# The last 128 output columns of a Mish layer: one cast and one store, or two of each by halves of the partitions

## The chip, the cores and the metric

The kernel runs on one core of a Trainium2 chip. The metric is the device time of one execution in microseconds (us). Each kernel is run several times, and the median is compared; beside these runs one execution is recorded by the hardware profiler.

## The reference

The layer takes `x` (2048 tokens by 512), `w1` (512 by 1792), `b1` (1792) and `w2` (1792 by 512), all in bf16:

```
h   = x @ w1 + b1
act = h * tanh(softplus(h))      # Mish
out = act @ w2                   # 2048 x 512, bf16
```

## The kernel before

The tokens are worked in four blocks of 512 (`BLOCKS`). For each block there are two stages on TensorE:

- First product (`mm1_step`, line 164). For each of 14 groups of 128 hidden features, four matrix products of 512 columns accumulate in one bank of PSUM, the accumulator memory of eight banks. ScalarE reads the bank, applies Mish with the bias and writes `a_sb` in bf16 (`mish`, line 170).
- Second product (`mm2`, line 197). For each of the four groups of 128 tokens in the block (index `i`, 0 to 15 over the whole kernel), 14 matrix products over the hidden features accumulate up to 512 output columns in one bank.

What follows a second product is `put`. One engine waits for the last of the 14 products, reads the bank and writes the result in bf16 to `o_sb`: VectorE at line 185, or, if the queue given is ScalarE's, ScalarE at line 182. Then a DMA is issued at line 189, from SP for VectorE's casts and from ScalarE for its own. SP and ScalarE have a DMA ring each (q1 and q10 in the profile). Every store adds 16 to the one semaphore `s_out`.

The order is written out by hand; there is no planner. All engines run their own instruction lists and wait on counting semaphores; `Stream.wait` leaves out a wait that is already known to be met. SP first issues all the loads (line 85) and then only the stores. ScalarE issues two loads at the start, then works 56 times Mish, then the last cast.

The last group of tokens, `i = 15`, is split: 512 - `LAST` = 416 columns go through VectorE and SP's ring, and the last `LAST` = 96 columns, with 14 products of their own in another bank, go through ScalarE and its ring. At the very end SP waits for all 17 stores (line 234).

Of the kernel before, what the change touches and what calls it, by code (L numbers as in the profile page):

```python
# [5 lines left out]
P = 128  # L6
WARM = (512,) * 5 + (128,) * 5
BLOCKS = (512, 512, 512, 512)
LAST = 96


class Stream:
# [20 lines left out]
def bass_standalone__dense_activation_mish__prompt_kernel(  # L33
# [8 lines left out]
    ACT = mybir.ActivationFunctionType  # L42
# [3 lines left out]
    _, S, D = x.shape  # L46
# [3 lines left out]
    x2, out2 = x[0], out[0]  # L50
# [5 lines left out]
    with ExitStack() as es:  # L56
        def sb(name, shape, t):
            return es.enter_context(nc.sbuf_tensor(name, shape, t))
# [12 lines left out]
        o_sb = sb("o_sb", [P, S // P, D], BF)  # L71
        ps = es.enter_context(nc.psum_tensor("ps", [P, 8, 512], F32))

        def sem(name):
            return es.enter_context(nc.semaphore(name))

        sp = Stream(nc.sync, None)
        pe = Stream(nc.tensor, sem("c_pe"))
        dve = Stream(nc.vector, sem("c_dve"))
        act = Stream(nc.scalar, sem("c_act"))  # L80
# [29 lines left out]
        out01 = out2[0:2 * P, :].rearrange("(p j) d -> p j d", j=2)  # L110
# [24 lines left out]
        free = [[] for _ in range(8)]  # L135
# [19 lines left out]
        def mm1_step(s, f, k, bank, j0=0, j1=None):  # L155
            j1 = BLOCKS[s] // P if j1 is None else j1
            lo, hi = j0 * P, j1 * P
            first = k == 0 and j0 == 0
            if first:
                pe.wait(*free[bank])  # L160
            pe.wait(t_w1[k, f])
            for j in range(starts[s] // P + j0, starts[s] // P + j1):
                pe.wait(t_cp[k] if j < 2 else t_xT[j])
            return nc.tensor.matmul(ps[:, bank, lo:hi], w1_sb[:, k, f * P:(f + 1) * P],  # L164
                                    xT[:, k, starts[s] + lo:starts[s] + hi], start=first,
                                    stop=(k == KT - 1 and hi == BLOCKS[s]))

        def mish(s, f, bank, t_mm):
            act.wait(t_b1c, t_mm)
            t = act.mark(act.eng.activation(a_sb[:, f, starts[s]:starts[s + 1]], ps[:, bank, 0:BLOCKS[s]], ACT.Mish,  # L170
                                            bias=b1_sb[:, f:f + 1]))
            t_mish[s, f] = t
            free[bank] = [t]

        s_out = sem("s_out")
        n_out = 0

        def put(i, lo, hi, bank, t_mm, q):
            nonlocal n_out
            if q is act:  # L180
                act.wait(t_mm)
                t = act.mark(act.eng.activation(o_sb[:, i, lo:hi], ps[:, bank, 0:hi - lo], ACT.Copy))  # L182
            else:
                dve.wait(t_mm)
                t = dve.mark(nc.vector.tensor_copy(o_sb[:, i, lo:hi], ps[:, bank, 0:hi - lo]))  # L185
            free[bank] = [t]
            q.wait(t)
            dst = out01[:, i, lo:hi] if i < 2 else out2[i * P:(i + 1) * P, lo:hi]
            q.eng.dma_start(dst, o_sb[:, i, lo:hi]).then_inc(s_out, 16)
            n_out += 1  # L190

        def mm2(i, lo, hi, bank, q=sp):
            s = max(b for b in range(len(BLOCKS)) if starts[b] <= i * P)
            pe.wait(*free[bank])
            for f in range(FT):
                pe.wait(t_w2[f], t_mish[s, f])
                mm = nc.tensor.matmul(ps[:, bank, 0:hi - lo], a_sb[:, f, i * P:(i + 1) * P], w2_sb[:, f, lo:hi],  # L197
                                      start=(f == 0), stop=(f == FT - 1))
            put(i, lo, hi, bank, pe.mark(mm), q)


        for n in WARM:
# [14 lines left out]
        for f in range(F0):  # L217
            for k in range(KT):
                mm = mm1_step(0, f, k, f, 2, 4)
            mish(0, f, f, pe.mark(mm))  # L220

        for s in range(len(BLOCKS)):
            for f in range(F0 if s == 0 else 0, FT):
                bank = f % 8 if s == 0 else 4 + f % 4
                for k in range(KT):
                    mm = mm1_step(s, f, k, bank)
                mish(s, f, bank, pe.mark(mm))
            for i in range(starts[s] // P, starts[s + 1] // P):
                if i < S // P - 1:
                    mm2(i, 0, D, i % 4)  # L230
                else:
                    mm2(i, 0, D - LAST, i % 4)
                    mm2(i, D - LAST, D, (i + 1) % 4, act)
        sp.eng.wait_ge(s_out, 16 * n_out)


# [26 lines left out]
```

## Time and profile before

| what | us |
|---|---|
| median of three runs | 105.71 |
| the three runs | 105.72, 105.71, 105.05 |
| the profiled execution, whole time | 104.98 |
| its span, first to last instruction | 103.7 |
| TensorE busy in the span | 100.9 (97%) |
| VectorE busy | 13.2 (13%) |
| ScalarE busy | 38.9 (38%) |
| TensorE's granted clock, mean | 1.000 |

The span is shorter than the whole time by what lies before the first and behind the last instruction that the profile shows. Rows of the profile name an engine by PE (TensorE), PEld (its weight loads), DVE (VectorE), ACT (ScalarE), POOL (GpSimd) and SP (SyncE); "SPq" and "ACTq" are DMA issues by the queues of SP and ScalarE. "L185" is line 185 of the kernel. "128x416 bf16<-128x416 f32" means 128 partitions by 416 elements, read as f32 and written as bf16. The time of a DMA issue is that of the issuing instruction; its "landing" is when its semaphore has been raised in full.

### The profile page before, as it was taken

The numbers are of one execution on the slowest core, as the hardware profiler recorded it, in microseconds if no ns is written. First come the engines' busy times: TensorE is split into PE (matmuls) and PEld (weight loads), VectorE is DVE, ScalarE is ACT, GpSimd is POOL, SyncE is SP. The second block draws the span as 40 slices with busy tenths as digits, with TensorE's granted clock in tenths as the row PEclk, the third lists the DMA queues.
The fourth block names the chain that finished last, engine by engine and source line by source line (L and its number), as shares of the span: only waits on it lengthen the run. The fifth ranks groups of instructions, "written<-read, shape, count | busy, mean of one in ns | idle before, by whom it ended". The sixth has DMA issues, their size and how long they took to land.

```text
span 103.7 us, 1167 instructions
## 1 busy us (share of the span) xinstructions
PE 100.9 (97%) x512; PEld 49.8 (48%) x512; DVE 13.2 (13%) x26; ACT 38.9 (38%) x58; POOL 0.7 (1%) x6
## 2 busy tenths in 40 slices
PE   6999999999999999999999999999999999999992
PEld 2788744444444444444444444444444444444451
DVE  0430000212220000022220000022211000021122
ACT  1305997000037777100007777400006777700000
POOL 2000000000000000000000000000000000000000
PEclk9999999999999999999999999999999999999999
DMA  1999995992110000011011000001111000001111
GB/s 54 355 303 354 350 254 123 231 241 69 51 45 6 0 6 0 0 51 47 4 51 51 0 0 0 9 0 51 51 51 51 0 0 0 0 6 51 51 51 51
DMA packets 12865, 7.94 MB, mean 77 GB/s; under 512 B 7868, under 2 KB 12220, under 8 KB 12860
## 3 DMA queue, kind: packets, MB, share of 16 engines
q1 hardware_dynamic: 12544, 7.58, 27.6%
q10 hardware_dynamic: 316, 0.29, 0.9%
q8 instruction: 4, 0.07, 0.3%
q14 instruction: 1, 0.01, 0.0%
HBM read 3.94 MB, written 2.10 MB: 58 GB/s over the span
## 4 chain that ended last, share of the span: by engine, by line
PE 97%; ACT 0%; issue 0%
PE ps L164 47%; PE ps L197 47%; PE ps L133 3%; PE ps L145 1%; ACT o_sb L182 0%
## 5 line engine op out<-in xcount | busy, mean ns | idle before, releaser
L170 ACT ACTIVATE a_sb<-ps,b_sb 128x512 bf16<-128x512 f32 x56 | 37.4, 692 | 49.6 <-PE ps L164 49.6
L164 PE MATMUL ps<-xT,w_sb 128*128 128x512 bf16 (+1 forms) x256 | 49.5, 355 | 0.0
L197 PE MATMUL ps<-w_sb,a_sb 128*128 128x512 bf16 (+2 forms) x238 | 49.0, 366 | 0.0
L164 PEld LDWEIGHTS ps<-xT,w_sb 128*128 128x128 bf16 x256 | 25.2, 99 | 23.5
L197 PEld LDWEIGHTS ps<-w_sb,a_sb 128*128 128x128 bf16 x238 | 22.7, 98 | 26.1
L185 DVE CAST o_sb<-ps 128x512 bf16<-128x512 f32 (+1 forms) x16 | 11.0, 685 | 84.5 <-PE ps L197 84.5
L182 ACT ACTIVATE o_sb<-ps 128x96 bf16<-128x96 f32 x1 | 0.2, 250 | 11.4 <-PE ps L197 11.4
L133 PE MATMUL ps<-const-bfloat16-1.0 128*128 128x512 bf16 (+1 forms) x10 | 2.8, 466 | 0.8 <-PEq L248 0.8
L133 PEld LDWEIGHTS ps<-const-bfloat16-1.0 128*128 128x128 bf16 x10 | 1.2, 139 | 2.2 <-issue 2.2
L127 ACT ACT_TABLE_LOAD x1 | 1.3, 1283 | 2.1 <-issue 2.1
L149 DVE COPY xT<-ps 128x256 bf16<-128x256 bf16 (+1 forms) x3 | 0.9, 336 | 3.1 <-PE ps L145 2.9
L145 PE MATMUL ps<-ident,x_nat 128*128 128x128 bf16 x8 | 1.0, 309 | 0.0
L211 DVE STREAM_TRANSPOSE b_t<-b_pad 32x32 bf16<-32x32 bf16 x4 | 0.8, 202 | 0.1
L145 PEld LDWEIGHTS ps<-ident,x_nat 128*128 128x128 bf16 x8 | 0.8, 139 | 0.1
L125 POOL TENSOR_SCALAR_AFFINE_SELECT ident<-ones 128x128 bf16<-128x128 bf16 x1 | 0.3, 292 | 0.1
L106 DVE MEMSET b_pad<- 32x64 uint32 x1 | 0.1, 112 | 0.9 <-PEq L248 0.9
L123 POOL MEMSET ones<- 128x128 bf16 x1 | 0.2, 204 | 0.3 <-POOLq L248 0.3
L208 DVE COPY b_pad<-b_nat 14x128 bf16<-14x128 bf16 x1 | 0.2, 182 | 0.0
L213 DVE CAST b_sb<-b_t 128x14 f32<-128x14 bf16 x1 | 0.2, 175 | 0.0
L248 POOL MEMSET const-bfloat16-1.0<- 128x1 bf16 x1 | 0.1, 101 | 0.0
L248 POOL MEMSET const-uint8-127<- 128x1 uint8 x1 | 0.1, 101 | 0.0
L248 POOL MEMSET const-float32-0.0<- 128x1 f32 x1 | 0.1, 98 | 0.3 <-issue 0.3
(1 smaller groups left out, 0.1 us busy)
## 6 DMA issues: line engine op xcount, KB each, us to landing
out_dram<-o_sb SPq DMA_DIRECT2D x15, 128.0 KB, 1.7
w_sb<-in_w_dram SPq DMA_DIRECT2D x1, 1152.0 KB, 11.7
w_sb<-in_w_dram SPq DMA_DIRECT2D x3, 256.0 KB, 4.3
w_sb<-in_w_dram SPq DMA_DIRECT2D x2, 384.0 KB, 5.3
w_sb<-in_w_dram SPq DMA_DIRECT2D x1, 640.0 KB, 7.2
x_nat<-in_x_dram SPq DMA_DIRECT2D x1, 256.0 KB, 2.6
w_sb<-in_w_dram ACTq DMA_DIRECT2D x1, 256.0 KB, 3.1
out_dram<-o_sb SPq DMA_DIRECT2D x1, 104.0 KB, 1.7
```

The costliest lines, as they stand in the source:

```text
L123: t_ones = pool.mark(pool.eng.memset(ones[:, :], 1.0))
L125: t_id = pool.mark(pool.eng.affine_select(ident[:, :], ones[:, :], pattern=[[1, P]], compare_op=ALU.is_equal, fill=0.0, base=0, channel_mu ...
L127: act.eng.preload_act_table(ACT.Mish)
L133: nc.tensor.matmul(ps[:, 7, 0:n], c_w, c_m[:, 0:n], start=True, stop=True)
L145: mm = nc.tensor.transpose(psb[:, (2 * i + j) * P:(2 * i + j + 1) * P], x_nat[:, j, k * P:(k + 1) * P], ident[:, :])
L149: t = dve.mark(nc.vector.tensor_copy(xT[:, ks[0]:ks[0] + n, 0:2 * P], psb[:, 0:2 * n * P].rearrange("p (k t) -> p k t", k=n)))
L164: return nc.tensor.matmul(ps[:, bank, lo:hi], w1_sb[:, k, f * P:(f + 1) * P], xT[:, k, starts[s] + lo:starts[s] + hi], start=first, stop=( ...
L170: t = act.mark(act.eng.activation(a_sb[:, f, starts[s]:starts[s + 1]], ps[:, bank, 0:BLOCKS[s]], ACT.Mish, bias=b1_sb[:, f:f + 1]))
L185: t = dve.mark(nc.vector.tensor_copy(o_sb[:, i, lo:hi], ps[:, bank, 0:hi - lo]))
L197: mm = nc.tensor.matmul(ps[:, bank, 0:hi - lo], a_sb[:, f, i * P:(i + 1) * P], w2_sb[:, f, lo:hi], start=(f == 0), stop=(f == FT - 1))
L211: t_b1t = dve.mark(nc.vector.transpose(b1_t[c * 32:(c + 1) * 32, :], b1_pad[:, c * 32:(c + 1) * 32]))
L248: nc = _bacc.Bacc("TRN2", target_bir_lowering=False, num_devices=1)
```

## The change

`LAST` becomes 128, so the last group of tokens is split into 384 and 128 columns. `put` now takes the casting engine, the issuing queue and a range of partitions. For the last 128 columns (`mm2_halves`) VectorE casts partitions 0 to 63 and SP stores them; ScalarE casts partitions 64 to 127 and stores them from its own ring. All other parts (`mm2_whole`) go through VectorE and SP as before. Each ring has a semaphore of its own, and at the end SP waits for its 17 stores and ScalarE for its one.

```
-LAST = 96
+LAST = 128
...
-        s_out = sem("s_out")
-        n_out = 0
-
-        def put(i, lo, hi, bank, t_mm, q):
-            nonlocal n_out
-            if q is act:
-                act.wait(t_mm)
-                t = act.mark(act.eng.activation(o_sb[:, i, lo:hi], ps[:, bank, 0:hi - lo], ACT.Copy))
-            else:
-                dve.wait(t_mm)
-                t = dve.mark(nc.vector.tensor_copy(o_sb[:, i, lo:hi], ps[:, bank, 0:hi - lo]))
-            free[bank] = [t]
-            q.wait(t)
-            dst = out01[:, i, lo:hi] if i < 2 else out2[i * P:(i + 1) * P, lo:hi]
-            q.eng.dma_start(dst, o_sb[:, i, lo:hi]).then_inc(s_out, 16)
-            n_out += 1
+        s_out = {sp: sem("s_out_sp"), act: sem("s_out_act")}
+        n_out = {sp: 0, act: 0}
...
-            put(i, lo, hi, bank, pe.mark(mm), q)
+            return pe.mark(mm)
+
+
+        def put(eng, q, i, a, b, lo, hi, bank, t_mm):
+            eng.wait(t_mm)
+            to, src = o_sb[a:b, i, lo:hi], ps[a:b, bank, 0:hi - lo]
+            t = eng.mark(eng.eng.activation(to, src, ACT.Copy) if eng is act else eng.eng.tensor_copy(to, src))
+            q.wait(t)
+            dst = out01[:, i, lo:hi] if i < 2 else out2[i * P:(i + 1) * P, lo:hi]
+            q.eng.dma_start(dst[a:b, :], to).then_inc(s_out[q], 16)
+            n_out[q] += 1
+            return t
+
+        def mm2_whole(i, lo, hi, bank):
+            free[bank] = [put(dve, sp, i, 0, P, lo, hi, bank, mm2(i, lo, hi, bank))]
+
+
+        def mm2_halves(i, lo, hi, bank):
+            t_mm = mm2(i, lo, hi, bank)
+            put(dve, sp, i, 0, P // 2, lo, hi, bank, t_mm)
+            put(act, act, i, P // 2, P, lo, hi, bank, t_mm)
...
-                    mm2(i, 0, D, i % 4)
+                    mm2_whole(i, 0, D, i % 4)
                 else:
-                    mm2(i, 0, D - LAST, i % 4)
-                    mm2(i, D - LAST, D, (i + 1) % 4, act)
-        sp.eng.wait_ge(s_out, 16 * n_out)
+                    mm2_whole(i, 0, D - LAST, i % 4)
+                    mm2_halves(i, D - LAST, D, (i + 1) % 4)
+        for q in (sp, act):
+            q.eng.wait_ge(s_out[q], 16 * n_out[q])
```

More of the change, by code (lines that the diff above doesn't have):

```diff
@@ L173, in mish, with mm2 @@
             free[bank] = [t]
-        s_out = sem("s_out")
-        n_out = 0
-        def put(i, lo, hi, bank, t_mm, q):
-            nonlocal n_out
-            if q is act:
-                act.wait(t_mm)
-                t = act.mark(act.eng.activation(o_sb[:, i, lo:hi], ps[:, bank, 0:hi - lo], ACT.Copy))
-            else:
-                dve.wait(t_mm)
-                t = dve.mark(nc.vector.tensor_copy(o_sb[:, i, lo:hi], ps[:, bank, 0:hi - lo]))
-            free[bank] = [t]
-            q.wait(t)
-            dst = out01[:, i, lo:hi] if i < 2 else out2[i * P:(i + 1) * P, lo:hi]
-            q.eng.dma_start(dst, o_sb[:, i, lo:hi]).then_inc(s_out, 16)
-            n_out += 1
-        def mm2(i, lo, hi, bank, q=sp):
+        s_out = {sp: sem("s_out_sp"), act: sem("s_out_act")}
+        n_out = {sp: 0, act: 0}
+        def mm2(i, lo, hi, bank):
             s = max(b for b in range(len(BLOCKS)) if starts[b] <= i * P)
```

## The prediction

> **What bounds the kernel now.** I read the summary page first: its table of engines, then the chain that ended last.
>
> ```profile
> span 103.7 us, 1167 instructions
> ...
> PE 100.9 (97%) x512; PEld 49.8 (48%) x512; DVE 13.2 (13%) x26; ACT 38.9 (38%) x58; POOL 0.7 (1%) x6
> ...
> PE 97%; ACT 0%; issue 0%
> ```
>
> TensorE is busy from the first microsecond to the last two, and 97% of the chain is TensorE. The change adds no matrix product and takes none away, so only the tail behind the last product can move. The chain in order of time names where the tail begins, and the timeline of the last microseconds shows it piece by piece (columns: start, length, then engine, line, operation):
>
> ```profile
> 89.62 12.14 PE ps L197 x70
> 101.75 0.02 issue
> 101.78 0.25 ACT o_sb L182
> ```
>
> ```profile
> 95.70 0.69 DVE L185 CAST o_sb<-ps 128x512 bf16<-128x512 f32 x1 [2.33 <-PE ps L197]
> 98.72 0.69 DVE L185 CAST o_sb<-ps 128x512 bf16<-128x512 f32 x1 [2.33 <-PE ps L197]
> 101.18 0.59 DVE L185 CAST o_sb<-ps 128x416 bf16<-128x416 f32 x1 [1.77 <-PE ps L197]
> 101.78 0.25 ACT L182 ACTIVATE o_sb<-ps 128x96 bf16<-128x96 f32 x1 [11.43 <-PE ps L197]
> 101.80 0.33 SPq L189 DMA_DIRECT2D out_dram<-o_sb  x1
> 102.06 0.37 ACTq L189 DMA_DIRECT2D out_dram<-o_sb  x1
> ```
>
> The reader should see two short chains. The 416 columns are cast by VectorE from 101.18 and stored from SP at 101.80; the last 96 are cast by ScalarE from 101.78 and stored from ScalarE's own ring at 102.06. Which one ends the kernel is in the list of DMA issues (last column: us from issue to landing), and SP's own wait list shows that it stands at the final wait:
>
> ```profile
> out_dram<-o_sb SPq DMA_DIRECT2D x15, 128.0 KB, 1.7
> out_dram<-o_sb SPq DMA_DIRECT2D x1, 104.0 KB, 1.7
> out_dram<-o_sb ACTq DMA_DIRECT2D x1, 24.0 KB, 1.6
> ```
>
> ```profile
> SPq L234 <- DMA out_dram<-o_sb: 1.5, 1, 1.5
> ```
>
> SP's store lands at 101.80 + 1.7 = 103.50, ScalarE's at 102.06 + 1.6 = 103.66; the span ends at 103.7. So the 96-column chain sets the end, by some 0.16 us, and the tail is 103.7 - 101.78 = 1.92 us, of which 1.6 is a store of only 24 KB. That is the whole stage that the change can touch: 1.8% of the time.
>
> **Part 1, the split 384 + 128 instead of 416 + 96.** Does TensorE finish at another time? The 14 products of 416 columns run from the release of the cast at 98.72 to that of the cast at 101.18: 2.46 us, 0.176 each. The 14 of 96 run from there to 101.78: 0.60, 0.043 each. That is (0.176 - 0.043)/320 = 0.416 ns a column, so 14 x 384 cost 14 x 0.162 = 2.27 and 14 x 128 cost 14 x 0.056 = 0.79, together 3.06: what 2.46 + 0.60 gave. The last product still releases its readers at 101.78. Term: 0.00. The cast of the wide part now begins 0.18 us sooner, at 101.00.
>
> For its length the groups kept apart by shape serve (busy, mean ns):
>
> ```profile
> L185 DVE CAST o_sb<-ps 128x512 bf16<-128x512 f32 x15 | 10.4, 691 | 82.7 <-PE ps L197 82.7
> L185 DVE CAST o_sb<-ps 128x416 bf16<-128x416 f32 x1 | 0.6, 592 | 1.8 <-PE ps L197 1.8
> L170 ACT ACTIVATE a_sb<-ps,b_sb 128x512 bf16<-128x512 f32 x56 | 37.4, 692 | 49.6 <-PE ps L164 49.6
> L182 ACT ACTIVATE o_sb<-ps 128x96 bf16<-128x96 f32 x1 | 0.2, 250 | 11.4 <-PE ps L197 11.4
> L208 DVE COPY b_pad<-b_nat 14x128 bf16<-14x128 bf16 x1 | 0.2, 182 | 0.0
> ```
>
> VectorE: (691 - 592)/96 = 1.03 ns a column, hence 559 ns for 384: done at 101.56, 0.22 us ahead of the last product. This cover matters, since VectorE now has a second cast to do at 101.78. SP issues the wide store at 101.59 (0.03 behind its cast, as 101.80 stands behind 101.77) and is free at 101.92, ahead of its second store. Even if the wide part were back at 416 columns, VectorE would be free at 101.77, just in time. Landing at 101.59 + 1.7 = 103.29, it is off the path.
>
> **Part 2, the last 128 columns by halves.** Removed: one ScalarE cast of 128 x 96 and its store of 24 KB. Added: a VectorE cast and a ScalarE cast of 64 partitions x 128 columns, and a store of 16 KB on each ring. No row shows a cast of half the partitions. VectorE by columns: 592 - 288 x 1.03 = 295 ns. Bounds: 182 (the smallest copy of 128 columns above, 14 partitions) and 592. I take 295, because the 14-partition copy is no shorter in proportion to its partitions. ScalarE: (692 - 250)/416 = 1.06 ns a column gives 284; bounds 250 and 284 (the slope mixes two functions). So the halves are ready at 102.07 (VectorE) and 102.06 (ScalarE), and their stores issue at 102.10 and 102.09, against 102.06 before. Term: **+0.04**, by the later one. Behind the waiting casts nothing is queued on either engine but the store and the end. Half the partitions buy no shorter cast; the extra 32 columns cost that term.
>
> **Part 3, the two small stores.** DMA activity in 40 slices of 0.05 us, from 99.4 on for a lone 128 KB store (issued at 99.44), then from 101.7 on for the last two stores together:
>
> ```profile
> 99.44 0.33 SPq L189 DMA_DIRECT2D out_dram<-o_sb  x1
> ```
>
> ```profile
> GB/s 0 0 0 0 0 0 0 0 0 0 0 0 0 0 0 0 0 123 225 348 348 451 389 369 226 123 21 0 0 0 0 0 0 0 0 0 0 0 0 0
> ...
> q1 hardware_dynamic: 144, 0.13, 18.8%
> ```
>
> ```profile
> GB/s 0 0 0 0 0 0 0 0 0 0 0 0 0 0 0 0 0 0 83 183 266 366 333 349 304 283 215 148 77 16 0 0 0 0 0 0 0 0 0 0
> ...
> q1 hardware_dynamic: 144, 0.11, 16.2%
> q10 hardware_dynamic: 144, 0.02, 6.3%
> ```
>
> The lone store moves bytes from 100.25 to 100.75, 0.81 behind its issue; its packets fill 18.8% of 2.0 us, 0.38, so 0.12 of the 0.50 is the engines' uneven start. It lands 0.4 behind the last byte. The small ScalarE store, issued at 102.06, starts at about 102.87 by the same 0.81 and the last byte goes at 103.20: 0.33, of which its own packets fill 6.3% of 2.0, 0.13, and the uneven start 0.12. Some 0.08 is left for sharing the engines with the 104 KB. In the changed kernel the wide store begins 0.21 sooner, moves bytes from 102.40 to about 102.87, and is nearly gone when the halves begin at 102.90. Each half has 64 rows of 256 B instead of 128 of 192. Passing one behind the other they fill at least the 0.13 and at most a third more, 0.17 (same row count, longer rows); side by side, half of that. I take them one behind the other, the dearer case, at its middle 0.15. With the start's 0.12 that is 0.27 instead of 0.33: **-0.06**. Bounds: -0.14 (side by side) and 0.00 (no sharing relieved).
>
> By the Trainium skill, "DMA: Bandwidth & Descriptors", section "Rules for kernel authors", two transfers to disjoint partition halves serialize, as both spread over the same 16 engines, and one full transfer is advised. By that rule the term stays at -0.06; were the halves independent it would be -0.14. No row of this run has two equal halves in flight.
>
> **Part 4, a semaphore per ring.** SP waits for 17 stores, ScalarE for one. This adds a wait at the end of ScalarE's queue with nothing behind it but the program's end. Term 0.00 while ScalarE's end is covered by SP's; without that cover see the third rival.
>
> **Sum:** 0.00 + 0.04 - 0.06 + 0.00 = -0.02 us. The profiled execution took 104.98 (span 103.7 and 1.28 around it), so 104.96 for it. That execution is 0.73 under the median of the runs, 105.71, whose spread is 105.05 to 105.72. The step of -0.02 is put on the median: **105.7**.
>
> **Rivals.** (1) *The two issues exclude each other.* The stores issue 0.01 apart, on SP and on ScalarE. If the second waits until the first is done, it is late by 0.33 (SP's issue in the timeline): 105.71 - 0.02 + 0.33 = 106.0. For it: ScalarE's issue took 0.37 where it overlapped SP's by 0.07. Against it, the start of the kernel:
>
> ```profile
> 0.80 0.39 SPq L85 DMA_DIRECT2D x_nat<-in_x_dram  x1
> ...
> 1.01 0.38 ACTq L85 DMA_DIRECT2D w_sb<-in_w_dram  x1
> ```
>
> There two issues overlapped by 0.18 and each lost only some 0.05. The Trainium skill, "Perfetto Trace Analysis", section "DMA Instruction — HWDGE (DVE, Sync)", has the descriptor generator shared and locked by one sequencer at a time; by a full lock this rival holds.
>
> (2) *Small stores land sooner.* If a lone small store pays only the 0.81 before its first byte and the 0.4 behind its last, with 0.06 to 0.15 of packets between, it lands in 1.27 to 1.36 instead of 1.6: 105.71 + 0.04 - 0.33 = 105.4, or 105.5. For it: 128 KB land in 1.7, so the fixed part is most. Against it: the 24 KB took 1.6, and its end came 0.46 behind the last byte, later than for the large one.
>
> (3) *ScalarE's closing work comes onto the path.* Before, ScalarE is done at 102.43, 1.27 us ahead of the span's end; with its own wait it ends with SP. Whatever it does after its last instruction, within the 1.28 outside the span, was hidden up to those 1.27. If it takes longer than SP's, the excess is added: up to 1.27, so 106.98; at half, 106.3. It decides from about 0.1 us of excess, and passes 1% from 1.06. For it: 1.28 us outside the span are unexplained. Against it: VectorE and TensorE were done two microseconds earlier too, and closing work common to all engines is already paid by the last, SP.
>
> (4) *The halves are not cast side by side.* If two engines cannot read one bank of the accumulators at once, the second half comes 0.28 later: 106.0. No row has two engines in one bank, so nothing speaks for or against but the many casts beside running products in other banks.
>
> **How the numbers follow.** Forecast 0.58, rivals 0.16, 0.14, 0.08 and 0.04. A measurement of this kernel tells about 1%, 1.06 us, from no change. Forecast and rivals 1, 2 and 4 all lie within it. Slower by over 1% is the upper part of the third: 0.04. Faster by over 1% needs rival 2 at its full 0.3 together with all three runs at the low end of the spread (-0.66): 0.02. The rest, 0.94, is the same. Range: from 104.9 (the lowest run, 105.05, less the 0.14 of part 3 at its best) to 106.1 (the highest, 105.72, and 0.33 of late issue). Left out: most of rival 3.
>
> **What would show it.** Right: VectorE casts 384 columns in 0.56 from 101.00; both 64 x 128 casts begin at 101.78, taking 0.30 and 0.28; stores issue at 102.09 and 102.10; the wide store lands near 103.3; the span stays 103.6 to 103.8 with 1.28 around it. Wrong: an issue or first byte on one ring 0.3 behind the other (rival 1); landings at 1.4 or less (2); an unchanged span with a longer time (3); casts one behind the other (4). A product row longer than 0.056 of spacing for 128 columns would break part 1.

## The result and the profile after

| | before | changed |
|---|---|---|
| median of 21 runs each, us | 105.05 (104.52 to 105.79) | 105.67 (105.25 to 106.41) |
| profiled execution, us | 104.98 | 105.53 |
| its span, us | 103.7 | 104.1 |
| time less span, over all runs, us | 1.20 to 1.32 | 1.36 to 1.47 |

The ratio is 1.0061 with a 95% interval of 1.0037 to 1.0085: the changed kernel is slower by 0.64 us, between 0.39 and 0.89. That is under 1%, yet clear of no change. The forecast was -0.02 us. Its 105.7 agrees with the measured 105.67 only by chance: it was put on a median of three runs, 105.71, which stood 0.66 above the median of the longer series. The step is what was forecast wrongly. (The time outside the span of the kernel before is taken from the 35 runs of the first series of experiments. Spans are kept to 0.1 us, so each time outside, and each tail below, is good to about 0.05.) The prediction took 1.06 us for the least that a measurement tells from no change; with 21 runs each it is about 0.25, so the miss shows. Of the experiments below, the profiled executions of kernels 1 and 5 stalled inside the span (607 and 276.5 us); of the first no row is used, of the second only rows behind its last product.

The timeline of the changed kernel's tail (start, length, engine, line, operation), and SP's last issue by itself, as the row at 101.53 merges both of SP's issues:

```profile
100.95 0.56 DVE L191 CAST o_sb<-ps 128x384 bf16<-128x384 f32 x1 [1.58 <-PE ps L183]
101.53 1.05 SPq L194 DMA_DIRECT2D out_dram<-o_sb  x2
101.73 0.27 ACT L191 ACTIVATE o_sb<-ps 64x128 bf16<-64x128 f32 x1 [11.43 <-PE ps L183]
101.73 0.28 DVE L191 CAST o_sb<-ps 64x128 bf16<-64x128 f32 x1 [0.22 <-PE ps L183]
102.03 0.56 ACTq L194 DMA_DIRECT2D out_dram<-o_sb  x1
```

```profile
102.04 0.55 SPq L194 DMA_DIRECT2D out_dram<-o_sb  x1
```

Up to the two issues everything stands where it was expected: the last product releases both casts at 101.73, they take 0.28 and 0.27, and the stores are issued at 102.04 and 102.03. Before, the one store issued at 102.06. But the issues, SP's and ScalarE's, now take 0.55 and 0.56 instead of 0.33 and 0.37. The list of DMA issues of this stretch (last column: us to landing), and the DMA activity in 40 slices of 0.05 us from 102.2 on, show what follows:

```profile
out_dram<-o_sb SPq DMA_DIRECT2D x1, 96.0 KB, 1.6
out_dram<-o_sb ACTq DMA_DIRECT2D x1, 16.0 KB, 2.0
out_dram<-o_sb SPq DMA_DIRECT2D x1, 16.0 KB, 1.8
```

```profile
GB/s 0 0 0 123 246 338 369 369 308 154 62 0 0 0 0 0 0 0 0 0 26 92 108 82 21 0 82 103 93 46 5 0 0 0 0 0 0 0 0 0
```

The slices show three separate hills. The wide store moves bytes from 102.35 to 102.75. Then nothing moves for 0.45 us. SP's half follows from 103.20, 1.16 behind its issue, and ScalarE's from 103.50, 1.47 behind. Before, the first byte came 0.81 behind. No hill touches another, so the engines that move the bytes are not what is short.

The tail, from the start of the casts that the last product releases to the end of the span, was 103.7 - 101.78 = 1.92 us and is 104.1 - 101.73 = 2.37. This measure is used for all kernels below, since the span alone also holds the start of the kernel, which varies: these casts start anywhere from 101.4 to 102.6 in the profiles of kernels 2 to 4 and 6 to 9. Outside the span the profiled executions add 105.53 - 104.1 = 1.43 after and 104.98 - 103.7 = 1.28 before, another 0.15. So 0.45 + 0.15 = 0.60 us are to be explained.

### The profile page after: what moved, and what is told of

It is laid out like the page before. It is cut to its first block, busy times and chain, and to the rows that moved or that the text cites. A ratio compares the mean times of both kernels' runs of the same rounds, so it can differ in the third digit from the quotient of the medians.

```text
span 104.1 us, 1170 instructions
## 1 busy us (share of the span) xinstructions
PE 100.9 (97%) x512; PEld 49.9 (48%) x512; DVE 13.4 (13%) x27; ACT 38.9 (37%) x58; POOL 0.7 (1%) x6
## 4 chain that ended last, share of the span: by engine, by line
PE 97%; DVE 0%; issue 0%
PE ps L164 47%; PE ps L183 46%; PE ps L133 3%; PE ps L145 1%; DVE o_sb L191 0%
## 5 line engine op out<-in xcount | busy, mean ns | idle before, releaser
L191 DVE CAST o_sb<-ps 128x512 bf16<-128x512 f32 (+2 forms) x17 | 11.2, 660 | 84.4 <-PE ps L183 84.4
```

What stands on the lines that cost most here:

```text
L191: t = eng.mark(eng.eng.activation(to, src, ACT.Copy) if eng is act else eng.eng.tensor_copy(to, src))
```

## The experiments

The medians, ratios and tails of all kernels in one table; "outside" is the time less the span, as the range over the runs. Series ran at different times, so the ratios to the kernel before, measured beside each, are what compares.

| kernel | median us | ratio to before, 95% | tail us | outside us |
|---|---|---|---|---|
| changed kernel | 105.67 | 1.0061 (1.0037 to 1.0085) | 2.37 | 1.36 to 1.47 |
| 1 only the wait per ring | 105.34 | 1.0006 (0.9981 to 1.0031) | not read | 1.35 to 1.46 |
| 2 SP waits for both | 105.66 | 1.0052 (1.0022 to 1.0082) | 2.40 | 1.20 to 1.30 |
| 3 ScalarE later | 105.59 | 1.0050 (1.0017 to 1.0083) | 2.41 | 1.36 to 1.45 |
| 4 half casts, one store from SP | 105.09 | 0.9970 (0.9941 to 0.9999) | 1.84 | 1.19 to 1.29 |
| 5 both halves from SP | 105.75 | 1.0052 (1.0016 to 1.0088) | 2.77 | 1.22 to 1.31 |
| 6 halves by columns | 105.68 | 1.0047 (1.0019 to 1.0074) | 2.66 | 1.20 to 1.47 |
| 7 96 and 32 rows | 105.39 (one run) | none | 1.99 | 1.39 |
| 8 one cast, one store from SP | 104.96 | 0.9982 (0.9952 to 1.0013) | 1.79 | 1.21 to 1.33 |
| 8 once more | 104.92 | 0.9981 (0.9947 to 1.0016) | 1.75 | 1.22 to 1.31 |
| 9 96 and 32 rows, SP waits | 105.23 | 1.0014 (0.9985 to 1.0043) | 1.95 | 1.22 to 1.34 |

Kernels 10 and 11, below, measure single stores; they have one run each, 105.24 and 105.42.

### 1 and 2: who ends last

The first theory had two parts: two issues at the same moment on two rings get in each other's way, and the closing behind the span grows when ScalarE ends last. The first two kernels test the second part alone, from both sides. Kernel 1 is the kernel before with

```
-        s_out = sem("s_out")
+        s_out = {sp: sem("s_out_sp"), act: sem("s_out_act")}
...
-        sp.eng.wait_ge(s_out, 16 * n_out)
+        for q in (sp, act):
+            q.eng.wait_ge(s_out[q], 16 * n_out[q])
```

> The kernel before with only the semaphore per ring and ScalarE's own wait at the end. Theory (ScalarE ending last lengthens the closing outside the span): span unchanged at 103.7, the time outside the span rises from 1.27 to about 1.41, so +0.14 us in the time. Rival (the closing does not care which engine ends last; the 1.41 after the change is chance): 1.27 outside, time as before.

Kernel 2 is the changed kernel with

```
-            q.eng.wait_ge(s_out[q], 16 * n_out[q])
+            sp.eng.wait_ge(s_out[q], 16 * n_out[q])
```

> The changed kernel, but SP waits for both semaphores and ScalarE for none. Theory: the two issues still collide, both at about 0.55 us, the span stays at 104.1, and the time outside it falls back from 1.41 to 1.27: about 0.14 us faster than the change, still 0.4 slower than before. Rival (closing does not depend on the engine): no difference from the change.

The time outside the span answers it without any overlap: 1.35 to 1.46 over the 12 runs of kernel 1, 1.20 to 1.30 over the 12 runs of kernel 2. Against the medians of the kernel before, 1.26, and of the changed kernel, 1.43, adding ScalarE's wait costs 0.14 (median 1.40) and taking it away gives 0.17 back (median 1.26): about 0.15. In the time itself 0.15 us is 0.14%, which the intervals cannot tell. Kernel 6, below, whose two stores land at nearly the same moment, has both values in one program: its runs fall into two groups, six from 1.20 to 1.30 and four from 1.39 to 1.47, which fits now one ring ending last and now the other; its profiled execution, in which SP's store landed last, has 1.30. The Trainium skill, "Runtime: NRT & Kernel Launch", section "The ~15µs preamble/postamble breakdown", gives 44 ns a hop for the barrier that passes from engine to engine ahead of a kernel. It gives no hop for the barrier behind the kernel; if that one's hops are as long, an estimate from the page makes 0.15 about three of them. No run here shows the hops.

### 3 and 4: is it two issues at one moment?

Kernel 3 delays ScalarE's store by one more cast into an unused tile:

```
+        spare = sb("spare", [P, LAST], BF)
...
+            act.wait(t_mm)
+            act.eng.activation(spare[P // 2:P, :], ps[P // 2:P, bank, 0:hi - lo], ACT.Copy)
             put(act, act, i, P // 2, P, lo, hi, bank, t_mm)
```

> The changed kernel with one more cast of the same half into an unused tile ahead of ScalarE's cast, so that ScalarE's store issues about 0.28 us behind SP's instead of beside it; more work on the path, and nothing else moved. Theory (two issues at the same moment get in each other's way): SP's issue back at 0.33 and its store landing in 1.6, ScalarE's issue at 0.37 to 0.40 from 102.33, landing in 1.6 to 1.7, so the span falls to about 103.95 in spite of the added cast. Rival (a store of 64 partitions is slow by itself): issues stay at 0.55, ScalarE's landing stays near 2.05, span about 104.4.

The timeline of its last microseconds for ScalarE, SP's last issue, and the landings:

```profile
101.49 0.27 ACT L207 ACTIVATE spare<-ps 64x128 bf16<-64x128 f32 x1 [11.43 <-PE ps L184]
101.67 0.26 ACT L192 ACTIVATE o_sb<-ps 64x128 bf16<-64x128 f32 x1
101.96 0.53 ACTq L195 DMA_DIRECT2D out_dram<-o_sb  x1
```

```profile
101.81 0.55 SPq L195 DMA_DIRECT2D out_dram<-o_sb  x1
```

```profile
out_dram<-o_sb SPq DMA_DIRECT2D x1, 16.0 KB, 1.8
out_dram<-o_sb ACTq DMA_DIRECT2D x1, 16.0 KB, 1.9
```

The span, 103.9, is what the theory said, and it misleads: the last product ended 0.24 sooner in this execution. The tail is 2.41, no shorter than the change's, and both issues still take 0.55 and 0.53. The two casts overlap by 0.09, so ScalarE's issue came only 0.15 behind SP's and the two were not fully apart. The test did not separate the theories as planned, but SP's issue gave no sign of relief. The later issue cost nothing: ScalarE's first byte again comes 0.29 behind SP's (0.30 in the changed kernel), so its store had been standing behind SP's anyway.

Kernel 4 keeps the split and the half casts and joins the stores; SP alone waits at the end:

```
+            for eng, a, b in ((dve, 0, P // 2), (act, P // 2, P)):
...
+                sp.wait(t)
+            sp.eng.dma_start(out2[i * P:(i + 1) * P, lo:hi], o_sb[:, i, lo:hi]).then_inc(s_out[sp], 16)
...
+        sp.eng.wait_ge(s_out[sp], 16 * n_out[sp])
```

> The changed kernel's 384 + 128 columns and its two half casts, but one store of all 128 partitions from SP that waits for both casts; ScalarE issues none and waits for none. Theory (collision of issues): SP's last issue at 102.05 takes 0.33, lands in 1.6 to 1.7, span 103.65 to 103.75, outside 1.27, time as before or up to 0.05 less. Rival (two engines reading one bank, or the split 384 + 128, is what costs): the span stays near 104.1.

Its cast, its last issue and that store's landing:

```profile
102.56 0.28 DVE L207 CAST o_sb<-ps 64x128 bf16<-64x128 f32 x1 [0.22 <-PE ps L183]
102.92 0.33 SPq L209 DMA_DIRECT2D out_dram<-o_sb  x1
```

```profile
out_dram<-o_sb SPq DMA_DIRECT2D x1, 32.0 KB, 1.5
```

Here too the span alone, 104.4, would have pleaded for the rival; the tail, 104.4 - 102.56 = 1.84, does not. With one store of 128 rows the tail is 0.53 below the change's, while the two half casts and the columns are the same. That clears the casts and the shared bank. The rule of the Trainium skill weighed in the prediction, one full transfer rather than two halves, is borne out by the result: 32 KB in one store land in 1.5, each 16 KB half in 1.8 and 2.0. Its reason, the halves sharing the engines, could at most put the second hill behind the first. It does not explain the 0.45 us ahead of the first hill, in which the engines move nothing.

### 5, 6 and 7: two rings, or 64 rows?

Kernel 5 takes the second ring away, with its wait; kernel 6 keeps both rings but gives each store all rows; kernel 7 changes the row counts.

```
-            put(act, act, i, P // 2, P, lo, hi, bank, t_mm)
+            put(act, sp, i, P // 2, P, lo, hi, bank, t_mm)
...
+        sp.eng.wait_ge(s_out[sp], 16 * n_out[sp])
```

> The changed kernel with both 64-row stores issued from SP, one behind the other; ScalarE casts its half, issues nothing and waits for none, so that no two issues are at work at once. Theory A (a store of 64 rows is slow by itself: long issue, late first byte): both issues at 0.55 us, first byte 1.2 behind the first issue, the second store issued near 102.6 and landing 1.7 to 1.8 later, span near 104.4. Theory B (two issues at one moment get in each other's way): both issues at 0.33, landings of 1.5 to 1.6, span near 104.0. Time outside the span 1.27 in both.

```
...
+                sp.wait(t)
+                act.wait(t)
+            mid = (lo + hi) // 2
+            for q, c, d in ((sp, lo, mid), (act, mid, hi)):
+                q.eng.dma_start(out2[i * P:(i + 1) * P, c:d], o_sb[:, i, c:d]).then_inc(s_out[q], 16)
...
```

> Casts by halves as in the changed kernel, but the two stores take all 128 rows of 64 columns each, issued at the same moment from SP and from ScalarE, when both casts are done. Theory A (64 rows are slow by themselves): issues near 0.33 and 0.37, landings of 1.5 to 1.8, span 103.6 to 103.9. Theory B (collision): both issues at 0.55 or more, first bytes 1.2 and 1.5 behind, span 104.1 or later, as twice the rows are to be described. Outside the span 1.41 in both.

```
-            put(dve, sp, i, 0, P // 2, lo, hi, bank, t_mm)
-            put(act, act, i, P // 2, P, lo, hi, bank, t_mm)
+            put(dve, sp, i, 0, 96, lo, hi, bank, t_mm)
+            put(act, act, i, 96, P, lo, hi, bank, t_mm)
```

> The changed kernel with 96 rows through VectorE and SP and 32 through ScalarE, instead of 64 and 64. Theory A, if the issue grows as the rows fall short of 128 (128 rows 0.33, 64 rows 0.55, the 14-row load of the bias 0.67): SP's issue about 0.44, ScalarE's about 0.62. If any count under 128 costs the same: 0.55 for both. Theory B (collision): both at 0.55, whatever the rows.

SP's two last issues in kernel 5, one view each, with no other ring at work:

```profile
272.84 0.55 SPq L194 DMA_DIRECT2D out_dram<-o_sb  x1
```

```profile
273.43 0.59 SPq L194 DMA_DIRECT2D out_dram<-o_sb  x1
```

The last two issues of kernel 6, on two rings, 0.06 apart:

```profile
102.12 0.38 ACTq L212 DMA_DIRECT2D out_dram<-o_sb  x1
102.18 0.33 SPq L212 DMA_DIRECT2D out_dram<-o_sb  x1
```

The last two of kernel 7, 0.01 apart, and their landings:

```profile
102.31 0.39 ACTq L194 DMA_DIRECT2D out_dram<-o_sb  x1
```

```profile
102.32 0.35 SPq L194 DMA_DIRECT2D out_dram<-o_sb  x1
```

```profile
out_dram<-o_sb SPq DMA_DIRECT2D x1, 24.0 KB, 1.5
out_dram<-o_sb ACTq DMA_DIRECT2D x1, 8.0 KB, 1.7
```

These three turn the theory over. Alone on one ring, 64 rows take 0.55. On two rings at the same moment, 128 rows take 0.33 and 0.38, and 96 and 32 rows 0.35 and 0.39. The collision costs an issue some 0.05 at most; the 64 rows are slow. None of the values expected for kernel 7 came (0.44 and 0.62, or 0.55 for both), so the issue does not simply grow as the rows fall short of 128.

Kernel 6's issues are what was asked of it, but it is as slow in time as the change, and its span missed the 103.9 at most that was expected. Two other things did that. Its edit also made ScalarE's cast wait for VectorE's, so the second cast begins 0.38 behind the first. And among its last stores stands a transfer of instructions, the list's queue q14, at 102.79 in the DMA activity (40 slices of 0.085 us from 101 on):

```profile
GB/s 0 0 0 0 0 0 0 0 0 0 0 0 54 235 407 307 145 9 0 0 0 96 0 24 131 156 52 14 11 0 0 0 0 0 0 0 0 0 0 0
...
q14 instruction: 1, 0.01, 0.6%
```

In the profiles of the kernel before, the changed kernel and kernel 7 that queue's one transfer comes between 65 and 67 us. A store's 16 on its semaphore arrive as sixteen steps. In the trace of kernel 6, fifteen of them are in by 103.65 for ScalarE's store and by 103.82 for SP's, and the last comes at 103.94 and 104.11, 0.29 later. Less the 0.38 and the 0.29, the tail of 2.66 would be about 2.0, that of kernel 7. That the transfer held up the last step is read from these times and was not tested.

Kernel 7's tail is 1.99. In one step, from 64 + 64 to 96 + 32 rows, it gave back 0.38 of the 0.45.

### 9, 10 and 11: the rows measured by themselves

Kernels 10 and 11 cut the stores of earlier token groups, which are off the path, into pieces, with one ring at work at a time. Of kernel 10:

```
+            if i == 4:
+                sp.eng.dma_start(out2[r + 0:r + 64, 0:512], o_sb[0:64, i, 0:512]).then_inc(s_out[sp], 16)
+                sp.eng.dma_start(out2[r + 64:r + 128, 0:512], o_sb[64:128, i, 0:512]).then_inc(s_out[sp], 16)
...
```

> A measurement, not a candidate: the last part as one ScalarE cast and one store from SP, and the stores of ten earlier token groups (4 to 13), which are off the path, cut into pieces of other rows and columns, all issued from SP one behind the other with no other ring at work: 64+64, 96+32, 112+16, 80+48, 72+56 and 124+4 rows of 512 columns, 64 rows of 384, 256 and 128 columns, 64 rows from partition 32 on. Theory A1 (64 rows alone are slow): issue 0.55 for every 64-row piece of any width, 0.33 to 0.39 for the others. Theory A2 (rows below 128 cost by their number): the issue rises as the rows fall, and 64 lies between 96 and 32. Theory B (only a second ring's issue at the same moment makes them long): 0.33 for all, as nothing else issues.

Its SP timeline has one row for each piece. Lines 204 and 205 are 64 + 64 rows of 512 columns, 208 and 209 are 96 + 32, 212 and 213 are 112 + 16, 216 and 217 are 80 + 48; 225 and 226 are 64 + 64 of 128 columns, followed by 227 with 128 rows; 230 is 64 rows from partition 32 on, followed by 231 and 232 with 32 rows each; 235 and 236 are 72 + 56:

```profile
45.47 0.56 SPq L204 DMA_DIRECT2D out_dram<-o_sb  x1
46.07 0.58 SPq L205 DMA_DIRECT2D out_dram<-o_sb  x1
48.49 0.36 SPq L208 DMA_DIRECT2D out_dram<-o_sb  x1
48.90 0.41 SPq L209 DMA_DIRECT2D out_dram<-o_sb  x1
51.51 0.32 SPq L212 DMA_DIRECT2D out_dram<-o_sb  x1
51.87 0.43 SPq L213 DMA_DIRECT2D out_dram<-o_sb  x1
54.53 0.32 SPq L216 DMA_DIRECT2D out_dram<-o_sb  x1
54.89 0.43 SPq L217 DMA_DIRECT2D out_dram<-o_sb  x1
...
72.67 0.47 SPq L225 DMA_DIRECT2D out_dram<-o_sb  x1
73.17 0.60 SPq L226 DMA_DIRECT2D out_dram<-o_sb  x1
73.81 0.59 SPq L227 DMA_DIRECT2D out_dram<-o_sb  x1
75.69 0.55 SPq L230 DMA_DIRECT2D out_dram<-o_sb  x1
76.28 0.58 SPq L231 DMA_DIRECT2D out_dram<-o_sb  x1
76.91 0.42 SPq L232 DMA_DIRECT2D out_dram<-o_sb  x1
78.71 0.35 SPq L235 DMA_DIRECT2D out_dram<-o_sb  x1
79.11 0.32 SPq L236 DMA_DIRECT2D out_dram<-o_sb  x1
```

Every store of 64 rows takes 0.47 to 0.60, wide or narrow, from partition 0, 32 or 64. And whatever is issued right behind one is long as well: 128 rows 0.59, 32 rows 0.58, while the second 32 rows, behind 32, take 0.42. That fits a slow part that is still at work when SP has let go of the instruction, so that the next issue waits for it; what it is, no row shows. The first byte is late here too: it comes 1.18 behind the issue of line 204, and 0.82 behind that of line 216. All other counts, where no 64 rows stand right ahead, stay at 0.43 or less. Theory A2 falls: 48 and 16 rows are no slower than 32. Theory B falls too.

Kernel 11, made in the same way, asks how sharp the count is, and whether ScalarE's ring has it.

> A measurement with pieces of other row counts, stores of groups 4 to 13 off the path: 40+88, 24+104, 8+120, 60+68, 63+65 and 32+96 rows from SP; 64+64 and 32+96 rows from ScalarE alone; 64 rows of two runs of 128 columns; 64+64 rows from SP once more. Theory A1 (64 rows alone are slow, on either ring): issue of 0.47 to 0.60 for the 64-row pieces and for what is issued right behind one, under 0.45 for all the others, from ScalarE as from SP. Rival 1: the slow count is a band around 64 (60, 63, 65, 68 slow too). Rival 2: a quirk of SP's ring (64 rows from ScalarE alone at 0.37 to 0.40).

Lines 216 and 217 are 60 + 68 rows, 220 and 221 are 63 + 65, 238 is 64 rows of two runs each, 243 and 244 are 64 + 64 again (SP's timeline); 228 and 229 are 64 + 64 and 232 and 233 are 32 + 96 from ScalarE alone (ScalarE's):

```profile
54.72 0.33 SPq L216 DMA_DIRECT2D out_dram<-o_sb  x1
55.09 0.30 SPq L217 DMA_DIRECT2D out_dram<-o_sb  x1
72.85 0.28 SPq L220 DMA_DIRECT2D out_dram<-o_sb  x1
73.17 0.32 SPq L221 DMA_DIRECT2D out_dram<-o_sb  x1
75.87 0.63 SPq L238 DMA_DIRECT2D out_dram<-o_sb  x1
...
94.00 0.50 SPq L243 DMA_DIRECT2D out_dram<-o_sb  x1
94.54 0.60 SPq L244 DMA_DIRECT2D out_dram<-o_sb  x1
```

```profile
69.83 0.54 ACTq L228 DMA_DIRECT2D out_dram<-o_sb  x1
70.41 0.60 ACTq L229 DMA_DIRECT2D out_dram<-o_sb  x1
```

```profile
97.03 0.34 ACTq L232 DMA_DIRECT2D out_dram<-o_sb  x1
97.41 0.43 ACTq L233 DMA_DIRECT2D out_dram<-o_sb  x1
```

It is 64 and not its neighbours, and it is the same on both rings. The first byte of line 228, from ScalarE with no other ring at work, comes 1.17 behind its issue; the 1.47 of the changed kernel is another 0.30. Why that count is slow, no run shows; it stays open. Loads were not tried.

Kernel 9 then takes both causes out of the changed kernel and leaves the rest: 96 and 32 rows, and SP waiting for both semaphores.

> The changed kernel with 96 and 32 rows instead of 64 and 64, and SP waiting for both semaphores. Theory (the loss is the slow 64-row stores plus the closing behind ScalarE): both causes are gone, the issues take 0.35 and 0.39, last cast to span end about 2.0 us (the change 2.39, before 1.93), 1.26 outside: within 0.1 us of the kernel before, 0.4 to 0.5 less than the change. Rival (two rings at one moment): stays 0.4 slower than before.

The ratio is 1.0014 (0.9985 to 1.0043), the tail 1.95, the time outside 1.22 to 1.34. The loss is gone as far as the measurement can tell, though two rings still issue at the same moment. The second store is not free even so: the tails of kernels 7 and 9 are 0.1 to 0.2 longer than those of kernels 4 and 8, which have one.

### 8: a version without either cause

```
-            put(dve, sp, i, 0, P // 2, lo, hi, bank, t_mm)
-            put(act, act, i, P // 2, P, lo, hi, bank, t_mm)
+            put(act, sp, i, 0, P, lo, hi, bank, t_mm)
...
-        for q in (sp, act):
-            q.eng.wait_ge(s_out[q], 16 * n_out[q])
+        sp.eng.wait_ge(s_out[sp], 16 * n_out[sp])
```

> 384 + 128 columns; the last 128 are cast whole by ScalarE and stored by one store of 128 rows from SP, behind a single wait; SP alone waits at the end. By either theory no slow store is left: ScalarE's cast takes 0.27 to 0.28, SP's issue 0.33 starts 0.03 behind it, lands in 1.5, time outside the span 1.26. That is 0.10 to 0.15 us less than the kernel before, and 0.05 less than the kernel with two half casts and one store, which needs two waits on SP.

Its last cast, SP's last issue, and the landing:

```profile
101.81 0.28 ACT L191 ACTIVATE o_sb<-ps 128x128 bf16<-128x128 f32 x1 [11.43 <-PE ps L183]
```

```profile
102.11 0.33 SPq L194 DMA_DIRECT2D out_dram<-o_sb  x1
```

```profile
out_dram<-o_sb SPq DMA_DIRECT2D x1, 32.0 KB, 1.5
```

The tail is 1.79. The cast of 128 partitions takes 0.28, as long as that of 64: halving the partitions had nothing to give. It was run once more:

> The kernel with one ScalarE cast of the last 128 columns and one store from SP once more, for its interval. Theory, from its tail of 1.79 us against 1.93 before with the same time outside the span: 0.13 us less than the kernel before, ratio 0.9985 to 0.9990. Rival: no difference, ratio 1.000.

Both series give 0.998, 0.2 us under the kernel before, but both intervals reach past 1 (1.0013 and 1.0016). It is well ahead of the changed kernel; that it beats the kernel before is likely by its tail and not shown by its times. Kernel 4, with the same single store, points the same way: its interval ends at 0.9999.

## Why the prediction was right or wrong

- **Part 1, the split: right.** The cast of 384 columns took 0.56 and began 0.78 ahead of the release of the last casts, which is 14 x 0.056; no time was gained or lost on TensorE.
- **Part 2, the casts: right.** 0.28 and 0.27 were measured against 0.295 and 0.284 worked out, side by side on one bank, and the issues follow 0.31 and 0.30 behind the release (0.32 and 0.31 worked out). Rival 4 is out.
- **Part 3, the stores: this step failed.** Its term was -0.06, from 0.81 to the first byte and from packets. It carried the issue of 0.33 and the 0.81, both read from stores of 128 rows, over to stores of 64 rows, and gave bounds only to the packets. The issue took 0.55, and the first byte came 1.16 behind on SP and 1.47 on ScalarE. From issue to the end of the span the last store needs 104.1 - 102.03 = 2.07 us, against 103.7 - 102.06 = 1.64 before: +0.43 where -0.06 stood. That the halves pass one behind the other was taken rightly.
- **Part 4, the wait per ring: the other miss.** 0.00 was worked out, as long as SP's end covers ScalarE's, and about 0.15 measured (kernels 1 and 2): ScalarE's store landed at 102.03 + 2.0 = 104.03, SP's at 102.04 + 1.8 = 103.84, so the cover was not there. Rival 3 had the mechanism and its place; of the 1.27 that it allowed, 0.15 came.
- **Rival 1** gave 106.0 by an issue that waits for the other. The second half's bytes do come 0.30 behind the first's, so a wait was there. But simultaneous issues of other row counts run side by side at a cost of 0.05 (kernels 6 and 7), and the first half was late too. In one thing the trace agrees with the shared and locked descriptor generator of the Trainium skill, cited there: what is issued behind 64 rows is held, on the same ring (issues of 0.58 to 0.60) and, it seems, on the other (1.47 to the first byte, where 64 rows alone have 1.17).
- **Rival 2** fails for the halves (1.8 and 2.0). A single store of 128 rows does land sooner than before, in 1.5 against 1.6.
- **The sum:** +0.45 in the tail and +0.15 behind it make 0.60, against 104.98 to 105.53 = 0.55 in the profiled executions (whose last product also ended 0.05 sooner) and 0.64 by the ratio.

## What to carry to other kernels

Where no row shows a shape of store, its issue and its first byte need bounds as well as its bytes; cutting some stores that are off the path into the new shape prices them all in one profile. When the end of a kernel is compared between single profiles, measure from the last release, not by the span. Which engine waits last can lengthen what lies behind the span, so a final wait is best left where it was.

## What the runs showed of the hardware

- A store of exactly 64 rows takes 0.47 to 0.63 us to issue on SP's or ScalarE's ring, against 0.26 to 0.43 for the other counts tried (4 to 128 rows, 60, 63, 65 and 68 among them), where no 64-row store stands ahead of them; its first byte comes some 0.35 later (1.16 to 1.18 behind the issue, against 0.81 and 0.82), and the issue right behind it is held too.
- One 128-row store is as slow: the first of the kernel before, issued at 21.65, 0.04 behind the end of a DMA transpose from the same ring, takes 0.58. So 64 rows are not all that holds an issue.
- Casts of 128 columns out of PSUM take the same 0.26 to 0.29 us for 32, 64, 96 or 128 partitions.
- The time outside the span is 1.19 to 1.34 us when SP ends last and 1.35 to 1.47 when ScalarE does.
